# Two linear-attention and gated-MLP layer pairs on one core: block sums asked for later, fold copies moved from VectorE to ScalarE

## The chip, the cores and the metric

The kernel runs on one core of one Trainium2 chip. The metric is the device time of one launch in microseconds, as the median of several launches. All five engines of the core take part: TensorE (PE, with its weight loads listed as PEld), VectorE (DVE), ScalarE (ACT), GpSimd (POOL) and the SyncE queue (SP), which issues most DMAs.

## The reference

The input `x` is 2048 tokens of 1024 features. Four residual layers follow one another, A, B, A, B, numbered 0 to 3 in the kernel; both A layers use the same weights, and so do both B layers.

```python
x = A_x
x = x + _A_ref(_layernorm(x), A_wqkv, A_wo)
x = x + _B_ref(_layernorm(x), B_W_gate, B_W_up, B_W_down)
x = x + _A_ref(_layernorm(x), A_wqkv, A_wo)
x = x + _B_ref(_layernorm(x), B_W_gate, B_W_up, B_W_down)
```

`_A_ref` is linear attention with 32 heads of 32: with `phi(t) = where(t > 0, t + 1, exp(t)) + 1e-6` it forms `kv = phi(k)^T v` per head, divides `phi(q) kv` by `phi(q) . sum(phi(k)) + 1e-6`, and multiplies by `wo`. `_B_ref` is `(relu(x Wg) * (x Wu)) Wd` with 3584 hidden features.

## The kernel before, in words

All tokens lie in SBUF as 16 tiles `x0` to `x15` of 128 tokens by 1024 features. A matmul is 128x128 by 128x512, and a unit of eight of them fills one PSUM bank.

**Layer A.** `project` (L436) makes q and k unit by unit. Once `kv` of all heads is known, it is multiplied into the output weights ahead of any query: `fold_wo(n)` (L630 to L651), n = 0 to 3, runs 16 small matmuls into four PSUM banks (`kv0`, `kv1` and two of the pool `ps3`) and then copies the four banks, i = 0 to 3, into the bf16 tiles `T`. The next call uses the same four banks, so its matmuls wait for these copies. Between two calls one or two `project` units of q run. `phi` (L370) turns a q unit into phi(q): three ACT instructions (L377 to L379) and one of DVE (L385), or one of ACT (L375) and two of DVE (L383, L385). At last `out_unit(sc, j, n2)` (L653) multiplies phi(q), transposed as `pqT`, with `T`: eight matmuls (L657) into a bank of the pool `ps`, which has four, and one DVE addition (L664) onto half of a token tile `x`. An out unit can start when the addition of the fourth unit before it has freed its bank. There are four quarters `sc` of eight out units.

**Between A and B.** While the out units of quarters 1 to 3 run, the first eight token tiles are normed for layer B: statistics (DVE, L154 and L159), 1/sigma (ACT, L161 and L162), a shift (DVE, L186), scaling to f16 (ACT, L188), and a DMA transpose issued by SP (`ln_turn`, L352) into `xnT`, two tiles of four token tiles each. The DMA transposes of `pqT` (L628) stand in the same SP queue, and each waits for GpSimd's scaling (L623).

**Layer B.** The gate and up products are computed with seven block products in place of eight. Four of the seven use sums and differences of blocks of the normed tokens. `sums_x(l, c, j)` (L815 to L827) makes them for one column block: for j = 0 to 3 it takes token tile j from the first `xnT` and token tile 4 + j from the second, and runs four DVE instructions (s1 to s4) into two tiles `s`. The first such product of layer B, `vg` (`mm(w, 5, ...)`, L866), reads the s1 part of all four j. The sums of the weights are read back from DRAM in layer 3, and made by DVE in layer 1 (`make_gu`, L784 to L792), which starts at the end of layer 0.

**What sets the order.** `later` is a list of tasks with due times, counted in ticks; `run` calls `tick` once behind each out unit. DVE and GpSimd have a hand-written order in this part (`manual_schedule`, L714): their instructions stand in the queue as the program text and the due tasks emit them. The order on PE, ACT and SP comes from a scheduler. In quarter `sc == 2` the sums of j = 0 to 3 are due 6, 9, 12 and 15 ticks ahead (L744 to L746). Ticks 1 to 8 follow the out units of quarter 2, ticks 9 to 16 those of quarter 3.

Of the kernel before, what the change touches and what calls it, by code (L numbers as in the profile page):

```python
# [89 lines left out]
class _Net:  # L90
# [318 lines left out]
    def layer_A(self, l, last_ln):  # L409
        nc, G, KT, D = self.nc, self.G, self.KT, self.D  # L410
        ring, later = self.ring, self.later
# [56 lines left out]
        def m_units(d):  # L468
            mt = self.temp([P, D], BF16, name=f"mt{l}_{d}")
            for h in range(H):  # L470
                ps = self.ps3.tile([P, NW], F32, tag="b")
                for t in range(self.ST):
                    nc.tensor.matmul(ps, lhsT=self.xn[l, t][:, d * P:(d + 1) * P],  # L473
                                     rhs=self.pk[l, t][:, h * NW:(h + 1) * NW],
                                     start=(t == 0), stop=(t == self.ST - 1))
                    if t == self.ST // 2 - 1:
                        later.tick()
                nc.scalar.activation(out=mt[:, h * NW:(h + 1) * NW], in_=ps, func=ACT.Copy)
                if h == H - 1:
                    later.at(2, lambda: kv_step(d, mt))  # L480
                later.tick()
# [122 lines left out]
        def z_chain(i):  # L604
            z_mult(*divmod(i, QT))
            if i < 10:
                later.at(2, lambda: z_chain(i + 1))

        def z_mult(sc, j):
            prod = ksum  # L610
            nc.gpsimd.tensor_tensor(out=prod, in0=pq_of[sc, j], in1=zrow, op=ALU.mult)  # L611
            later.at(2, lambda: z_sum(prod, sc, j))
# [17 lines left out]
        def fold_wo(n):  # L630

            n2, a = divmod(n, H)
            if n2 == 0:
                T.append(self.slot(f"T{l}_{a}", [P, 4, D]))
            ps = [pool.tile([P, NW], F32, tag=tag, name=f"fold{l}_{n}_{i}") for i, (pool, tag) in
                  enumerate(((self.kvp, "kv0"), (self.kvp, "kv1"), (self.ps3, "b"), (self.ps3, "b")))]
            wo = ring.get((l, f"o{n2}"))
            for b in range(R):
                g = a * R + b
                for i in range(R):  # L640
                    e = slice(i * HD, (i + 1) * HD)
                    nc.tensor.matmul(ps[i][b * HD:(b + 1) * HD, :], lhsT=kvT[e, g, e],
                                     rhs=wo[e, g, :], start=True, stop=True,
                                     tile_position=(i * HD, b * HD))
            for i in range(R):
                g = a * R + i
                dst = T[g // 4][:, g % 4, n2 * NW:(n2 + 1) * NW]
                if g % 2 or (l and g % 4):
                    nc.scalar.activation(out=dst, in_=ps[i], func=ACT.Copy)
                else:  # L650
                    nc.vector.tensor_copy(out=dst, in_=ps[i])  # L651
# [16 lines left out]
        def column_major(f, q):  # L668
            return [lambda j=j, c=c: f(q, j, c) for c in range(H) for j in range(QT)]

        def row_major(f, q):
            return [lambda j=j, c=c: f(q, j, c) for j in range(QT) for c in range(H)]

        def run(*lists):

            n = max(len(u) for u in lists)
            for i in range(n):
                for u in lists:
                    if i < len(u):
                        u[i]()  # L680
                        later.tick()
# [32 lines left out]
        with self.tc.manual_schedule(engines={mybir.EngineType.DVE, mybir.EngineType.Pool}):  # L714
            q3 = row_major(q_unit, self.NQ - 1)
            out0 = column_major(out_unit, 0)
            if l == 0:
                ring.free_before((l, "v0"))
                later.at(5, z_row)
                later.at(7, lambda: z_chain(0))  # L720
                for d in range(KT):
                    m_units(d)
            else:
                ring.load_to(ring.index((l, "v1")) + 1)
                m_products(q3.pop(0))
                q3.insert(0, lambda: None)
                later.at(1, lambda: self.behind(ring.last, self.bring_back, range(self.NS)))
                for t in range(self.NS, self.ST, 2):
                    later.at(10 + t, lambda t=t: self.behind(self.last_turn, self.bring_back, (t, t + 1)))

            def with_fold(u, i):
                return lambda: (u(), fold_wo(i // 2) if i % 2 == 0 else None)

            run(q3[:2])
            run([with_fold(u, i) for i, u in enumerate(q3[2:] + out0[:1])])
            run(out0[1:3])
            ring.free_slowly((l, "o0"), later, 2)
            for i in range(11, self.ST):
                later.at(1 + 3 * (i - 11), lambda i=i: z_mult(*divmod(i, QT)))
            run(out0[3:])  # L740
            for sc in range(1, self.NQ):
                if sc < 3:
                    self.ln_later(last_ln, sc - 1, 0, 3, 2)
                if sc == 2:  # L744
                    for j in range(QT):
                        later.at(3 * j + 6, lambda j=j: self.sums_x(last_ln, 0, j))  # L746
                if sc == 3 and l == 0:
                    for w in "gu":
                        later.at(8, lambda w=w: self.make_gu(ring.get((last_ln, 0, w, 0)), w, 0))
                run(row_major(out_unit, sc))  # L750
# [313 lines left out]
```

## Time and profile before

| what | before |
|---|---|
| time, median of 3 | 1482.26 us (1481.64 to 1482.26) |
| span of the profiled execution | 1482.7 us |
| PE busy | 1471.9 us, 99% |
| DVE busy | 868.5 us, 59% |
| ACT busy | 517.5 us, 35% |
| POOL busy | 283.8 us, 19% |
| mean granted TensorE clock | 0.999 |
| fold copies, ACT (L649) | 20, median 596 ns |
| fold copies, DVE (L651) | 12, median 681 ns |
| additions of out units, DVE (L664) | 64, median 680 ns |
| block sums, DVE (L824 to L827) | 16 each, about 420 ns each |

The folds of layer 0 end near 175 us and its out units near 237 us of the span. Those of layer 2 run from 900 to 914 us, and its out units from 911.5 to 971.5 us. In a list of instructions in order of time, a row gives the start, the duration, engine, line and operation, output and inputs and a count; the bracket behind it is the time that the engine stood idle before it and what it then waited for.

### The profile page before, as it was taken

Reading aid. Unit: us, or ns where it says so; the run is one execution under the profiler, and the core shown is the slowest. Engines: PE = TensorE matmul, PEld = TensorE weight load, DVE = VectorE, ACT = ScalarE, POOL = GpSimd, SP = SyncE. Lnnn points to the kernel's source line nnn. Section 1 sums busy time; section 2 is a strip of 40 time slices with the busy share of each in tenths; the row PEclk is TensorE's granted clock in tenths of the full one; section 3 lists DMA queues with packets and bytes.
Section 4 is the critical chain, followed back from the end, with each engine's and each line's share of the span. In section 5 each row is a group of like instructions: output and inputs, shape, how many; then the busy total and the mean of one; then the engine's idle time right before and its main releaser. Section 6 shows DMA issues by size and latency. Waiting matters only on the chain.

```text
span 1482.7 us, 18649 instructions
## 1 busy us (share of the span) xinstructions
PE 1471.9 (99%) x7007; PEld 668.5 (45%) x7007; DVE 868.5 (59%) x1491; ACT 517.5 (35%) x927; POOL 283.8 (19%) x190
## 2 busy tenths in 40 slices
PE   9999999999999999999999999999999999999999
PEld 4444444444444444444444444444444444444444
DVE  8995787666594433356379867874445433434632
ACT  5752323333330333340067524343333203333300
POOL 1356540111100011110023475401111000111000
PEclk9999999999999999999999999999999999999999
DMA  9855538444458954445833019984444688444461
GB/s 281 215 169 178 118 58 248 156 143 156 160 182 245 339 180 131 148 131 192 265 100 71 1 36 266 255 266 142 139 145 134 186 245 267 142 142 146 150 208 43
DMA packets 316060, 251.33 MB, mean 170 GB/s; under 512 B 105536, under 2 KB 291136, under 8 KB 315072
## 3 DMA queue, kind: packets, MB, share of 16 engines
q1 hardware_dynamic: 306000, 229.80, 53.2%
q10 hardware_dynamic: 9968, 20.32, 3.6%
q8 instruction: 55, 0.90, 0.3%
q14 instruction: 37, 0.30, 0.1%
HBM read 190.84 MB, written 34.60 MB: 152 GB/s over the span
## 4 chain that ended last, share of the span: by engine, by line
PE 86%; DVE 6%; issue 1%; DMA 0%; ACT 0%; DVEq 0%; ACTq 0%
PE yg L851 10%; PE dy L935 10%; PE yu L851 10%; PE ps L436 7%; PE dv L935 7%; PE dx L935 7%; PE xu L851 6%; PE xg L851 6%; PE ps L473 4%; PE vg L851 3%; PE vu L851 3%; PE zu L851 3%; PE zg L851 3%; PE ps L657 3%; PE my L534 1%; DVE x L664 1%
## 5 line engine op out<-in xcount | busy, mean ns | idle before, releaser
L851 PEld LDWEIGHTS <-w 128*128 128x128 f16 (+1 forms) x3136 | 306.7, 98 | 370.7 <-DVE w L789 1.1
L889 POOL TENSOR_TENSOR h<-m5u,m5g 128x512 f16<-128x512 f32 x56 | 71.2, 1271 | 814.5 <-DVE m5u L885 803.6
L436 PE MATMUL ps<-w,xnT 128*128 128x512 bf16 x1024 | 223.9, 379 | 0.5 <-DVE pq L385 0.3
L935 PEld LDWEIGHTS <-h 128*128 128x128 f16 x1120 | 109.6, 98 | 132.1
L882 DVE TENSOR_TENSOR zg<-yg,m5g 128x512 f32<-128x512 f32 x56 | 39.2, 699 | 204.2 <-PE yg L851 204.2
L436 PEld LDWEIGHTS <-xnT 128*128 128x128 bf16 x1024 | 99.4, 98 | 120.8 <-issue 2.6
L657 PE MATMUL ps<-T,pqT 128*128 128x512 bf16 x512 | 113.2, 383 | 3.1 <-DVE x L664 3.1
L851 PE MATMUL yg<-s,w 128*128 128x512 f16 x448 | 115.1, 379 | 0.0
L851 PE MATMUL xg<-xnT,w 128*128 128x512 f16 x448 | 115.0, 379 | 0.0
L851 PE MATMUL xu<-xnT,w 128*128 128x512 f16 x448 | 115.0, 379 | 0.0
L851 PE MATMUL yu<-s,w 128*128 128x512 f16 x448 | 115.0, 379 | 0.0
L859 ACT ACTIVATE m5g<-m5g 128x512 f32<-128x512 f32 x56 | 35.2, 629 | 200.2 <-DVE m5g L885 200.2
L935 PE MATMUL dy<-w,h 128*128 128x512 f16 x448 | 98.0, 379 | 0.0
L935 PE MATMUL dx<-w,h 128*128 128x512 bf16 x448 | 97.3, 379 | 0.0
L611 POOL TENSOR_TENSOR kvc<-pq,kvc 128x1024 f32<-128x1024 bf16 x32 | 70.4, 2199 | 71.0 <-DVE den L616 56.8
L657 PEld LDWEIGHTS <-pqT 128*128 128x128 bf16 x512 | 50.3, 99 | 65.1 <-issue 6.3
L154 DVE BATCH_NORM_STATS2 stats<-x 128x6 f32<-128x512 f32 (+1 forms) x120 | 76.6, 672 | 1.9 <-DMA x<-in_A_x_dram 1.6
L161 ACT ACTIVATE rstd<-mv,eps 128x1 f32<-128x1 f32 x64 | 18.2, 290 | 164.8 <-DVE mv L159 164.8
L455 POOL TENSOR_TENSOR kvc<-kvc,slab 128x512 f32<-128x512 f32 x46 | 58.3, 1274 | 75.1 <-DVE slab L385 57.3
L862 DVE TENSOR_TENSOR h<-yu,r 128x512 f16<-128x512 f32 x56 | 38.7, 692 | 56.3 <-PE yu L851 56.3
L885 DVE TENSOR_TENSOR m5u<-yu,m5u 128x512 f32<-128x512 f32 x56 | 38.7, 692 | 54.0 <-PE yu L851 52.9
L868 ACT ACTIVATE m5g<-vg 128x512 f32<-128x512 f32 x56 | 33.4, 597 | 98.5 <-PE vg L851 71.0
(127 smaller groups left out, 1982.7 us busy)
## 6 DMA issues: line engine op xcount, KB each, us to landing
w<-in_B_W_gate_dram SPq DMA_DIRECT2D x56, 512.0 KB, 5.9
w<-in_B_W_up_dram SPq DMA_DIRECT2D x56, 512.0 KB, 4.8
w<-td SPq DMA_DIRECT2D x32, 896.0 KB, 4.7
w<-in_B_W_down_dram SPq DMA_DIRECT2D x24, 896.0 KB, 5.0
w<-tg SPq DMA_DIRECT2D x42, 512.0 KB, 6.9
w<-tu SPq DMA_DIRECT2D x42, 512.0 KB, 5.7
w<-in_A_wqkv_dram SPq DMA_DIRECT2D x10, 1024.0 KB, 8.1
away<-x SPq DMA_DIRECT2D x16, 512.0 KB, 4.0
```

The costliest lines, as they stand in the source:

```text
L154: self.nc.vector.bn_stats(out=stats[:, c, :], in_=src[:, c * fmax:(c + 1) * fmax])
L436: nc.tensor.matmul(by_row(ps), lhsT=self.xnT[l, l_q][:, kt, j * P:(j + 1) * P], rhs=w[:, kt, :].rearrange("p (b i d) -> p i b d", i=R, d=H ...
L455: nc.gpsimd.tensor_tensor(out=ksum[:, cols], in0=ksum[:, cols], in1=pk, op=ALU.add)
L473: nc.tensor.matmul(ps, lhsT=self.xn[l, t][:, d * P:(d + 1) * P], rhs=self.pk[l, t][:, h * NW:(h + 1) * NW], start=(t == 0), stop=(t == sel ...
L611: nc.gpsimd.tensor_tensor(out=prod, in0=pq_of[sc, j], in1=zrow, op=ALU.mult)
L657: nc.tensor.matmul(ps, lhsT=pqT[sc][:, g, j * P:(j + 1) * P], rhs=T[g // 4][:, g % 4, n2 * NW:(n2 + 1) * NW], start=(g == 0), stop=(g == G ...
L851: nc.tensor.matmul(ps, lhsT=W[w][m][:, k, :], rhs=A[m][:, k, :], start=start and k == 0, stop=k == 3, skip_group_check=True)
L862: self.last_put = nc.vector.tensor_tensor(out=h[:, b, :], in0=ps, in1=R.pop(b), op=ALU.mult)
L882: nc.vector.tensor_tensor(out=Z[w], in0=Y[w], in1=V[w], op=ALU.add)
L885: nc.vector.tensor_tensor(out=V[w], in0=Y[w], in1=V[w], op=ALU.add)
L889: nc.gpsimd.tensor_tensor(out=h[:, 3, :], in0=V["u"], in1=V["g"], op=ALU.mult)
L935: nc.tensor.matmul(banks[j], lhsT=A(k)[:, j * P:(j + 1) * P], rhs=w[:, i, :], start=start and k == 0, stop=k == self.U - 1, skip_group_che ...
```

## The change

Two edits. The first concerns where the copies of the folded blocks run. In layer 0 nothing changes: odd g on ScalarE, even g on VectorE. In layer 2 (`l` is 2) VectorE had g = 0 and g = 4, which is one of the four copies of each call of `fold_wo`; now all sixteen are on ScalarE. It is meant to take the copies out of VectorE's queue.

The second asks for the sums of blocks later, in both A layers: at ticks 8, 11, 13 and 16 in place of 6, 9, 12 and 15. It is meant to give the DMA transposes more time to land before VectorE reaches the instructions that read them.

```diff
@@ fold_wo
-                if g % 2 or (l and g % 4):
+                if l or g % 2:
                     nc.scalar.activation(out=dst, in_=ps[i], func=ACT.Copy)
                 else:
                     nc.vector.tensor_copy(out=dst, in_=ps[i])
@@ layer_A
                 if sc == 2:
                     for j in range(QT):
-                        later.at(3 * j + 6, lambda j=j: self.sums_x(last_ln, 0, j))
+                        later.at((8, 11, 13, 16)[j], lambda j=j: self.sums_x(last_ln, 0, j))
```

In VectorE's queue the sums of j = 0 and j = 1 move behind two more additions (L664) and a shift (L186), those of j = 2 and j = 3 behind one more addition. The sums of j = 3 now stand behind the last addition of all. In layer 0 one instruction of `make_gu` for the second pair of weight tiles (L789 on `w10`) now stands between s1 and s2 of j = 3, and those of the first pair (`w8`) behind s4. On PE the scheduler's order at the head of layer B changes: in layer 3 it was `vg` first, and is now four matmuls of `xg`, two of `xu`, then `vg`; in layer 1 it was `xg`, `xu`, `vg`, and is now `xg`, `xu`, the second four of `xg`, three of the second four of `xu`, then `vg`. On ACT the last third of a phi (L379) now stands behind an exponential (L375) ahead of the second call's copies, and in SP's queue the transpose of token tile 6 moves ahead of weight loads.

## The prediction

> **What bounds the kernel now.** I first read the page's busy shares: PE is busy 99% of the span, so a change can win only where PE stands still or runs at a reduced clock. So the next view is PE's waits, summed over the whole span (columns: total us, times, longest).
>
> ```profile
> PE ps L657 <- DVE x L664: 3.1, 2, 2.4
> PE fold L642 <- DVE T L651: 1.5, 1, 1.5
> PE vg L851 <- DVE w L789: 0.2, 1, 0.2
> ```
>
> Besides waits at the start and two of 0.3 and 0.5 us, that is all: three places, and both edits aim at them. The timeline of PE shows where each lies.
>
> ```profile
> 226.82 10.52 PE L657 MATMUL ps<-T,pqT 128*128 128x512 bf16 x48 [0.70 <-DVE x L664]
> 239.30 1.04 PE L851 MATMUL vg<-s,w 128*128 128x512 f16 x4 [0.24 <-DVE w L789]
> ...
> 904.33 3.63 PE L436 MATMUL ps<-w,xnT 128*128 128x512 bf16 x16
> 909.42 0.44 PE L642 MATMUL fold<-w,kvc 32*32 32x512 bf16 x16 [1.46 <-DVE T L651]
> ...
> 913.71 43.34 PE L657 MATMUL ps<-T,pqT 128*128 128x512 bf16 x200
> 959.44 12.19 PE L657 MATMUL ps<-T,pqT 128*128 128x512 bf16 x48 [2.39 <-DVE x L664]
> 971.47 1.03 PE L851 MATMUL vg<-s,w 128*128 128x512 f16 x4
> ```
>
> Two things are to be seen: the brackets sum to 0.70 + 0.24 + 1.46 + 2.39 = 4.79 us, and the 48 matmuls behind the longest wait are slow. Before it 200 take 43.34 us, 0.2167 each; the 48 take 971.47 - 959.44 = 12.03 us, where 48 x 0.2167 = 10.40. That is 1.63 us more. The table of windows shows why; its columns are window, length, PE busy and count, granted clock, DMA share, GB/s.
>
> ```profile
> 955.00:957.00 2.00, 2.00 (x10) 1.00 1.00 191
> 957.00:960.00 3.00, 0.61 (x3) 0.91 0.92 176
> 960.00:962.00 2.00, 2.00 (x7) 0.50 1.03 290
> 962.00:964.00 2.00, 2.00 (x9) 0.79 1.27 256
> 964.00:966.00 2.00, 2.00 (x11) 1.00 1.11 271
> ```
>
> The clock was halved for some 3 us after the stop. Why DVE was late shows in its timeline.
>
> ```profile
> 224.61 0.42 DVE L824 TENSOR_TENSOR s<-xnT 128x512 f16<-128x512 f16 x1 [1.61 <-DMA xnT<-xnb]
> ...
> 953.35 0.21 DVE L159 BATCH_NORM_AGGREGATE mv<-stats 128x2 f32<-128x12 f32 x1
> 957.23 0.43 DVE L824 TENSOR_TENSOR s<-xnT 128x512 f16<-128x512 f16 x1 [3.67 <-DMA xnT<-xnb]
> ...
> 958.71 0.68 DVE L664 TENSOR_TENSOR x<-x,ps 128x512 f32<-128x512 f32 x1
> ```
>
> The sums of j = 0 stand at the head of DVE's queue, waiting for a transpose, and the addition that would free a bank stands behind them. The DMA is not what bounds the out units: it is what DVE waited for at the wrong place.
>
> **What the Trainium skill says.** "TensorE: Matmul & The Clock Gate", section "Architectural detail", of the Trainium skill says that DVE and ACT queues are strict first in, first out. The trace agrees: at 957.05 PE had four finished units, DVE idled 3.67 us, and none was added. The same page, section "What's actually happening", says that PE drops to half clock after about 3.4 us of idling, in free-running windows, and needs about as long to come back. Here 2.39 us were enough for 0.50, so the phase of the window matters. The skill's "SBUF — State Buffer", section "Who interferes with whom", says that DVE's two-port forms and GpSimd lock each other out of a shared port pair. I use this only to understand why an L383 at 906.10 lasted 1.87 us where others last 0.42 (GpSimd was busy from 905.77 to 909.95); it held up the copy that the fold waited for.
>
> **The fold copies (layer 2).** Removed from DVE: 4 x 0.68 us; added to ACT: 4 x 0.52 us (three in a row took 1.56 at 905.85). Off DVE nothing is gained directly, since DVE isn't the bound there; what counts is the last copy before each next call. Before, PE was ready for the third call at 907.96 and DVE's copy ended at 909.36. After, the second call's four copies follow each other on ACT. Before, ACT's L377 stood at 903.44, then L378, L379, L375, and three copies from 905.85 to 907.41. The extra copy of the first call moves this by 0.52, and the extra one of the second adds 0.52, so the last ends at about 908.5. The third call then starts when its first bank is free, at about 908.1, and ends at about 908.8 where it ended at 909.79: a gain of 0.9 us. Bounds: 1.46 if ACT keeps up, 0.4 if the reordered L375 waits for its unit and pushes the copies. The second call may wait 0.1 us for the first's fourth copy, which is within that. Behind ACT's copies stand the exponentials of the next q units; DVE's phi then comes about 1 us later at L385 of 905.55, but the banks it frees are needed by PE no sooner than 908.8. The fourth call had 3.5 us of PE work between: hidden.
>
> **The sums in layer 2.** At 953.56 DVE now takes two additions whose units PE had ended at 951.85 and 953.58 (counting back 1.733 us a unit from 957.05), and a shift. It reaches the sums at about 955.0, still waits for the landing at 957.2, and is through at 958.7. By then PE has two freed banks to fill, until 957.05 + 2 x 1.73 = 960.5, and the next addition ends at 959.3. So the 2.39 us go, and with them the stop that cost 1.63 of clock. Further down I ran DVE's new order by the durations of the old rows (0.60 per addition with overlap, 1.45 per four sums, 1.4 per statistics): each addition ends 0.9 to 1.8 us before PE wants its bank. The shift of token tile 6 comes at 954.2 where it was at 959.30, so its transpose can be issued at 958, not 960.81; that of tile 7 at about 962.8, not 965.59.
> The new wait is at the end. PE ends its units at 957.05 + 10.40 = 967.45; the last addition ends at 968.1, s1 of j = 3 at 968.55. PE first has `xg` x4 and `xu` x2, 6 x 0.216 = 1.3 us, and wants `vg` at 968.75: just met. The landing of tile 7, 3.2 to 6.6 us after issue with a median of 4.3 in this stretch, falls at 966 to 969.4, most likely 967.1, ahead of the 968.1 at which DVE asks. If the fold's 0.9 us come off PE but not off the DMA-paced transposes, `vg` waits up to 0.5. I take off 0.3 us. Net: 2.39 + 1.63 - 0.3 = 3.7 us.
>
> **The sums in layer 0.** The same turn removes 0.70: DVE runs two additions from 223.0 in its 1.6 us of idling. PE reaches layer B at 236.5 in place of 237.18. There DVE is the bound for a moment, and one L789 (0.60) for the second weight pair now stands ahead of the first pair's: last addition to 237.1, s1 237.5, L789 on `w10` 238.1, s2 to s4 239.2, L789 on `w8` at 239.8. PE has 15 matmuls of raw products until 239.7, then waits 0.1 for `vg`, 0.2 for the two L789 and L791 of the up weights, and 0.2 for the zg addition. So of 0.70 + 0.24, 0.5 come back: net 0.4, between 0 and 0.9.
>
> **Moved at no cost.** The other sums and shifts in both layers have the same count and durations; they are hidden behind PE's units. Weight loads of layer 3 come up to 1.2 us later in SP's queue, but `w103` was issued at 958.09 and isn't used until some 12 us into layer B. Behind this, layer B has no PE wait on weights or DMA, so the gain stays to the end.
>
> Sum: 0.9 + 3.7 + 0.4 = 5.0 us, so 1482.26 - 5.0 = 1477.2 us.
>
> **Rivals.** (1) Everything is as above, but the launches that are timed didn't have the clock drop: the profiled one has it, and the windows run freely. Then the 1.63 isn't there to win: 1477.2 + 1.6 = 1478.8. For it: 2.39 us is short of the 3.4 that the skill gives. Against it: the three times lie within 0.6 us, so no launch differs from another by 1.6. (2) The waits move: tile 7 lands at the late end, 969.4, `vg` idles about 1.1 us, the fold wins only 0.4, layer 0 nothing: 0.4 + 4.0 - 1.1 - 0.8 more in banks = 2.5, so 1479.8. For it: the DMA share is over 1.0 in the whole stretch. (3) It becomes slower: the sums of j = 3, now behind the last addition, hold up the start of both layers B by some 3 us each, each followed by a halved clock (1.6), while the removed waits give back only 4.8 and 1.6: 2 x 4.6 - 6.4 = +2.8, so about 1485.3. For it: the first product needs all four j. Against it: the scheduler put raw products ahead of `vg`, and landing had over 1 us to spare before.
>
> **How the numbers follow.** The forecast has 0.58, rival 1 0.20, rival 2 0.15, rival 3 0.07. The bound of 0.2% is 3.0 us, at 1479.3 and 1485.2. Faster: all of the forecast, nearly all of rival 1 and little of rival 2, 0.77. Within: most of rival 2 and a part of rival 3, 0.17. Slower: 0.06. The range goes from 1475.6 (all waits gone: 4.79 + 1.63 = 6.4, and some noise) to 1480.4 (beyond rival 2).
>
> **What would show it.** In PE's waits, L657 on L664 should be gone, L642 on T down to about 0.5 us or less and now on ACT. The 48 matmuls ahead of layer 3 should take 10.4 us with the clock at 1.00. DVE should still wait about 2 us for `xnT` in layer 2, to nobody's harm. `vg` of layer 3 should wait less than 0.5 us. I am wrong if PE waits for `vg` by more than a microsecond, or if the clock still drops.

## The result, and the profile after

The changed kernel takes 1478.26 us (median of 6 launches, 1477.22 to 1479.06) against 1482.30 us before (6 launches, 1481.64 to 1483.07). The ratio is 0.9971, with a 95% interval of 0.9958 to 0.9984: 4.0 us less, 0.29%. A second set of five launches (e4) gave 0.9968 (0.9955 to 0.9980), 1477.27 us. The forecast was 1477.2 us.

The spans of the two traces differ by more than the times do, 1482.7 - 1476.4 = 6.3 us. That difference is the main thing to be explained. The answers of the trace come first.

PE's waits of the changed kernel (total us, times, longest): the three rows shown of before are gone. Of what is left, these are the longest; they lie at the start of the kernel and, for L473, at 109 us in layer 0.

```profile
PE idle L246 <- DVE e L243: 1.3, 1, 1.3
PE ps L473 <- DVE slab L385: 0.5, 1, 0.5
PE tp L286 <- DVE x L168: 0.3, 1, 0.3
```

PE's timeline of the changed kernel, folds and out units of layer 2:

```profile
902.99 0.58 PE L642 MATMUL fold<-w,kvc 32*32 32x512 bf16 x16
903.50 3.63 PE L436 MATMUL ps<-w,xnT 128*128 128x512 bf16 x16
907.06 0.70 PE L642 MATMUL fold<-w,kvc 32*32 32x512 bf16 x16
...
911.62 53.70 PE L657 MATMUL ps<-T,pqT 128*128 128x512 bf16 x243
965.16 1.03 PE L851 MATMUL xg<-xnT,w 128*128 128x512 f16 x4
966.02 0.59 PE L851 MATMUL xu<-xnT,w 128*128 128x512 f16 x2
966.45 1.03 PE L851 MATMUL vg<-s,w 128*128 128x512 f16 x4
```

The third call comes right behind its q units, at 907.06. It takes 0.70 us where a call that waits for nothing takes 0.44: with the last of the four copies ending at 907.29 it starts on banks that are free and waits inside for the last, as forecast. The out units run through in one piece, and `vg` follows the raw products without a gap. The windows (window, length, PE busy and count, granted clock, DMA share, GB/s) show the clock at 1.00 where it had been 0.50:

```profile
957.00:960.00 3.00, 3.00 (x16) 1.00 0.89 199
960.00:962.00 2.00, 1.95 (x10) 1.00 1.05 384
```

DVE's timeline of the changed kernel has the wait for the transpose still in it, to nobody's harm, and what I had not valued enough, the shift of token tile 7 (L186 at 958.72) AHEAD of the sums of j = 1:

```profile
954.53 0.43 DVE L824 TENSOR_TENSOR s<-xnT 128x512 f16<-128x512 f16 x1 [1.65 <-DMA xnT<-xnb]
...
958.72 0.21 DVE L186 TENSOR_SCALAR shift<-mv,rstd 128x1 f32<-128x1 f32 x1
...
959.44 0.42 DVE L824 TENSOR_TENSOR s<-xnT 128x512 f16<-128x512 f16 x1
...
965.96 0.42 DVE L824 TENSOR_TENSOR s<-xnT 128x512 f16<-128x512 f16 x1
```

ACT's timeline of the changed kernel: the four copies of the second call end at 907.29. L375 didn't wait for its unit.

```profile
904.15 0.58 ACT L375 ACTIVATE e<-ps 128x512 f32<-128x512 f32 x1
...
905.24 2.05 ACT L649 ACTIVATE T<-fold 128x512 bf16<-128x512 f32 x4
```

### The profile page after: what moved, and what is told of

Read it like the earlier page. It is cut to its first block, busy times and chain, and to the rows that moved or that the text cites. A ratio compares the mean times of both kernels' runs of the same rounds, so it can differ in the third digit from the quotient of the medians.

```text
span 1476.4 us, 18611 instructions
## 1 busy us (share of the span) xinstructions
PE 1468.0 (99%) x6965; PEld 667.7 (45%) x7007; DVE 864.9 (59%) x1487; ACT 518.9 (35%) x931; POOL 283.8 (19%) x190
## 4 chain that ended last, share of the span: by engine, by line
PE 91%; DVE 2%; issue 1%; ACT 0%; DVEq 0%
PE yg L851 10%; PE yu L851 10%; PE dy L935 10%; PE ps L436 8%; PE ps L657 7%; PE dv L935 7%; PE dx L935 7%; PE xu L851 6%; PE xg L851 6%; PE ps L473 4%; PE vg L851 3%; PE zu L851 3%; PE zg L851 3%; PE vu L851 3%; PE my L534 1%; PE mv L534 1%
## 5 line engine op out<-in xcount | busy, mean ns | idle before, releaser
L935 PEld LDWEIGHTS <-e 128*128 128x128 f16 x448 | 43.8, 98 | 52.9
```

The costliest lines, as they stand in the source:

```text
L935: nc.tensor.matmul(banks[j], lhsT=A(k)[:, j * P:(j + 1) * P], rhs=w[:, i, :], start=start and k == 0, stop=k == self.U - 1, skip_group_che ...
```

## The experiments

To compare traces I cut PE's time at four marks: the first fold call of layer 0, the first and the fourth fold call of layer 2, and the `vg` of layer 3's second weight pair. "Head" is what lies between the first two (it contains the sums of layer 0), "folds" the next stretch, "tail" the last (it contains the sums of layer 2). All in us. Spans are not compared as a whole, because launches differ by up to 3.3 us before the first mark (it lies at 169.2 to 172.5 us in the traces, whatever the edit). The clock column counts launches whose mean granted clock over the whole span was 0.999 or less, so that a half-rate stretch is somewhere in them; it does not say where.

| kernel | head | folds | tail | time ratio to before (95%) | launches with a clock drop anywhere |
|---|---|---|---|---|---|
| before, as traced ahead of the prediction | 729.31 | 13.40 | 70.21 | | |
| e1 before again | 729.54 | 13.40 | 68.24 | 0.9999 (0.9991 to 1.0007) | 1 of 13 |
| e2 fold copies only | 729.52 | 12.25 | 68.53 | 0.9987 (0.9981 to 0.9994) | 1 of 21 |
| e3 sums only | 728.21 | 13.40 | 65.99 | 0.9978 (0.9969 to 0.9986) | 0 of 12 |
| changed kernel | 728.54 | 12.19 | 66.00 | 0.9971 (0.9958 to 0.9984) | 0 of 6 |
| e4 changed again | 728.49 | 12.26 | 65.99 | 0.9968 (0.9955 to 0.9980) | 0 of 5 |
| e5 j = 0 at tick 5, layer 2 | 729.28 | 13.39 | 71.19 | 1.0022 (1.0014 to 1.0030) | 12 of 14 |
| e6 j = 0 at tick 7, layer 2 | 729.38 | 13.40 | 68.49 | 0.9999 (0.9991 to 1.0007) | 2 of 13 |
| e7 j = 0 at tick 8, layer 2 | 729.35 | 13.40 | 67.83 | 1.0001 (0.9991 to 1.0011) | 4 of 14 |
| e8 changed, one copy, j = 3 at 15 | 728.20 | 12.87 | 66.36 | 0.9981 (0.9973 to 0.9989) | 4 of 13 |
| e9 j = 0 and 1 later, layer 2 | 729.33 | 13.40 | 66.23 | 0.9986 (0.9979 to 0.9992) | 1 of 21 |
| e10 j = 1 later, layer 2 | 729.58 | 13.39 | 67.90 | 1.0002 (0.9994 to 1.0010) | 2 of 13 |
| e11 j = 0 and 3 later, layer 2 | 729.51 | 13.40 | 66.82 | 0.9989 (0.9982 to 0.9996) | 0 of 21 |
| e12 changed, j = 3 at 15 in layer 0 | 728.20 | 12.25 | 65.99 | 0.9966 (0.9954 to 0.9979) | 0 of 5 |

### Was the traced launch of before like the timed ones? (e1)

> The kernel before, unchanged, launched often, to see span and clock of each launch. Theory A (the halved clock after the 2.39 us stop comes only in some launches): most launches have a span near 1480.4 us (1482.3 less the 1.85 us by which time exceeds span elsewhere) at clock 1.000, a few have 1482 to 1483 us at 0.999. Theory B (the clock drops in every launch): all launches have spans near 1482.5 us at 0.999, and the 2.3 us between the traced span difference (6.3) and the timed one (4.0) has another cause.

Theory A holds. Of the 146 launches of the kernel before in these comparisons, on three chips, 19 had the clock drop (1 of 13 and 3 of 40, 6 of 44, 9 of 49); the median spans of the comparison launches were 1480.5, 1480.9 and 1480.6 us. There had been a sign of it: the launch that was profiled ahead of the prediction took 1484.57 us, 2.3 us above the median of the three timed ones, and its span (1482.7) alone exceeds that median, while in every launch of these comparisons the time is 1.7 to 1.9 us longer than the span. PE's timeline of e1 has the stop, but shorter, and another wait at the head of layer 3 that the first trace did not have:

```profile
957.43 10.52 PE L657 MATMUL ps<-T,pqT 128*128 128x512 bf16 x47 [1.42 <-DVE x L664]
968.45 1.04 PE L851 MATMUL vg<-s,w 128*128 128x512 f16 x4 [0.50 <-DVE s L824]
```

So the tail costs 68.24 us in this launch and 70.21 in the one that the prediction was made from. The difference, 1.97 us, is 0.97 of a longer stop and 1.63 of half clock, less the 0.50 at `vg`; 0.1 is left over. It is most of the 2.3 us by which the traced difference exceeds the timed one; the rest (0.3 us) is within the spread of the launches.

The 19 launches need not have lost their clock in layer 2. In the traced launch of e6, which is one of those with the drop, the half rate lies at 8.6 to 12.0 us of the span, behind a stop of 1.97 us at the start of the kernel, and the clock stayed at 1.00 in layer 2. So at most 19 of 146 had it behind the stop in layer 2; the launch lists alone can't say how many.

The traces do show which stop is followed by half clock. In all 14 the granted clock changes only on a grid of 3.413 us. In the trace of before it changes at 7.12 us (to full), 959.44 (to half), 962.86 (to full) and, after the last matmul, at 1481.68 (to half): 279, 1 and 152 steps apart. Below are windows cut on that grid around the longest stop, first of before, then of e10 (a later experiment with a stop of 1.72 us):

```profile
956.03:959.44 3.41, 1.02 (x5) 1.00 0.99 182
959.44:962.85 3.41, 3.41 (x9) 0.50 0.95 293
```

```profile
954.39:957.80 3.41, 1.70 (x8) 1.00 0.93 174
957.80:961.21 3.41, 3.41 (x17) 1.00 1.04 299
```

In before the whole stop of 2.39 us falls into one window, and the next runs at half clock. In e10 PE idles 1.71 us of its window, and the next runs at full clock. Over all windows of the 14 traces, from the first change of the clock to the last, each in which PE idled 2.03 us or more is followed by half clock (17 of them, 14 behind the last matmuls of the kernel), and none in which it idled 1.72 us or less. By these figures a stop of 1.42 us as in e1 could not halve the clock wherever it fell.

### Each part alone (e2, e3, e4)

```diff
# e2: fold copies only
-                if g % 2 or (l and g % 4):
+                if l or g % 2:
# e3: sums only
-                        later.at(3 * j + 6, lambda j=j: ...)
+                        later.at((8, 11, 13, 16)[j], lambda j=j: ...)
# e4: both
```

> Only the copies of the second layer's folds move to ScalarE; sums are due as before. The theory of two separate edits: PE's wait of L642 on L651 goes, about 1.2 us less than before (1481.1), and the waits for the transposes stay at 0.7 and about 2.4 us, since the chain that issues the transposes moves along with PE. Rival (the transposes are paced by DMA traffic that does not move): PE comes to the sums 1.2 us earlier and waits 1.2 us longer, 3.6 us in layer 2, and the time is that of before.

> Only the due times of the sums change; VectorE keeps its fold copies. Theory: PE's waits of L657 on L664 go in both layers, L642 on L651 stays at 1.46 us, the clock stays at 1.00; from the traces 2.39 + 0.2 + 0.8 = 3.4 us, and 1.6 us more in those launches of before that had the halved clock: timed 1478.9 by theory A (drop in few launches), 1477.3 by theory B (in all).

> Both edits, the changed kernel unchanged, to be compared on the same chip. If the two edits add up: gain of the fold alone plus gain of the sums alone, about 4.2 us by theory A, 1478.1.

The parts add up. The folds alone shorten their stretch by 13.40 - 12.25 = 1.15 us and leave the tail at 68.5, 0.3 us longer than in e1; the rival, in which PE only meets the transposes sooner, would have put 1.15 onto the tail. The transposes moved with PE: the sums of j = 0 started 1.2 us earlier than in e1 (954.03 for 955.23), PE's longest wait on L664 was 1.58 for 1.42. The sums alone take 1.3 us off the head and 2.25 off the tail against e1. Times: -1.9, -3.3 and -4.7 us of 1482.3, with intervals of about 0.9 us or more to either side. From the traces, against e1, the changed kernel is about 1.0 (head) + 1.14 to 1.21 (folds) + 2.25 (tail) = 4.4 to 4.5 us shorter.

### How far ahead the sums of j = 0 may stand (e5, e6, e7)

Layer 2 alone, all other due times as before:

```diff
-                        later.at(3 * j + 6, lambda j=j: ...)
+                        later.at((5 if l and j == 0 else 3 * j + 6), lambda j=j: ...)   # e5; 7 in e6, 8 in e7
```

> The kernel before, but the sums of j = 0 in layer 2 are due one out unit EARLIER (tick 5, not 6); all else as before. Theory (the additions behind the waiting sums set PE's stop; one out unit of 1.73 us for each tick): the stop of L657 on L664 grows from 1.4 to 2.4 us to about 3.2 to 4.1 us, the clock falls to half behind it in most launches (0.999 in the launch list), and the time is 1.7 to 3.4 us above before: 1484.0 to 1485.7. Rival (the length of the stop is set by the landing alone, or the clock drop is chance): time within 0.5 us of before, clock 1.000 in nine of ten launches as before.

> The kernel before, but the sums of j = 0 in layer 2 are due one out unit later (tick 7); all else as before. Theory: one addition more ahead of the sums frees one bank, worth 1.73 us, so the stop of 1.4 to 2.4 us shrinks to 0 to 0.7, the clock stays at 1.00, and time is 1.4 to 2 us below before: 1480.5. A second step (tick 8) then has little left to win. Rival (both out units are needed): the stop stays above 1 us.

> The kernel before, but the sums of j = 0 in layer 2 are due two out units later (tick 8), as in the changed kernel; j = 1 to 3, layer 0 and the folds as before. Theory (only the wait at j = 0 costs time): the whole gain of the sums in layer 2, about 2.2 us, so 1480.1; the shift of token tile 6 comes earlier too, and with it the late landing of tile 7, so layer 3's first vg doesn't wait. Rival (the later j count too): less than half of it, with PE waiting for the sums of j = 1 to 3.

One tick earlier behaved as the theory said: a stop of 3.42 us, half clock behind it, 12 of 14 launches with a drop where before had 6 of 44 on the same chip, and 3.3 us more time. PE's timeline of e5, and its windows:

```profile
959.46 13.86 PE L657 MATMUL ps<-T,pqT 128*128 128x512 bf16 x56 [3.42 <-DVE x L664]
```

```profile
958.00:960.00 2.00, 0.54 (x2) 0.84 0.90 169
960.00:962.00 2.00, 2.00 (x7) 0.50 0.94 286
```

Later did not. With j = 0 alone at tick 8, just as in the changed kernel, the stop is gone and yet no time is gained (ratio 1.0001; the tail of the trace is 0.4 us shorter than in e1). The wait has moved to the head of layer 3, as the rival had it. PE's timeline of e7, then DVE's:

```profile
912.45 53.70 PE L657 MATMUL ps<-T,pqT 128*128 128x512 bf16 x248
967.82 1.04 PE L851 MATMUL vg<-s,w 128*128 128x512 f16 x4 [1.67 <-DVE s L824]
```

```profile
954.87 0.43 DVE L824 TENSOR_TENSOR s<-xnT 128x512 f16<-128x512 f16 x1 [1.17 <-DMA xnT<-xnb]
...
958.38 0.37 DVE L824 TENSOR_TENSOR s<-xnT 128x512 f16<-128x512 f16 x1
...
960.40 0.21 DVE L186 TENSOR_SCALAR shift<-mv,rstd 128x1 f32<-128x1 f32 x1
...
967.34 0.42 DVE L824 TENSOR_TENSOR s<-xnT 128x512 f16<-128x512 f16 x1 [2.19 <-DMA xnT<-xnb]
```

Between the landing of token tile 4 (954.87) and the shift of token tile 7 (960.40) stand two sets of sums. From that shift it takes 6.9 us of scaling and transpose until the sums of j = 3 can start. At tick 7 (e6) the same waiting is spread out: 0.43 and 0.45 us among the out units and 1.14 at `vg`, 2.02 in all where e1 had 1.42 + 0.50 = 1.92.

The theory that the prediction shares with e6 and e7 falls here. One tick earlier the missing bank does lengthen the loss (e5). From tick 6 on, the additions behind the sums of j = 0 set where PE waits, but no longer how much it waits in all. A chain through DVE is then proposed as what sets that; the next three runs test it: landing of tile 4, sums of j = 0, addition, statistics of tile 7, sums of j = 1, addition, shift of tile 7, scaling, transpose, sums of j = 3, `vg`.

### What shortens the chain (e9, e10, e11)

```diff
-                        later.at(3 * j + 6, lambda j=j: ...)
+                        later.at((8, 11, 12, 15)[j] if l else 3 * j + 6, lambda j=j: ...)   # e9
+                        later.at((6, 11, 12, 15)[j] if l else 3 * j + 6, lambda j=j: ...)   # e10
+                        later.at((8, 9, 12, 16)[j] if l else 3 * j + 6, lambda j=j: ...)    # e11
```

> The kernel before, with j = 0 at tick 8 and j = 1 at tick 11 in layer 2 only (j = 2 and 3 at 12 and 15 as before). Revised theory: what bounds this stretch is a chain on VectorE from the landing of token tile 4 over the sums of j = 0, the statistics and the shift of token tile 7, its scaling, its transpose and the sums of j = 3 to vg; the sums of j = 1 (1.45 us) stand inside it before the shift. So vg's wait of 1.67 us (j = 0 alone) falls to about 0.2, no stop among the out units, clock 1.00 in nearly all launches: time 1.6 us below before. Rival (j = 1 is of no account, vg waits for the DMA): vg still waits over 1 us and the time is that of before.

> The kernel before, with only j = 1 at tick 11 in layer 2 (j = 0 at 6, j = 2 and 3 at 12 and 15). Revised theory: the stop of 1.4 us among the out units stays, since the sums of j = 0 stay ahead of the additions, and vg's wait (0.5) goes: 0.5 us or less below before. Rival (the chain is all that counts): the full 1.5 us are gained with j = 1 alone.

> The kernel before, with j = 0 at tick 8 and j = 3 at tick 16 in layer 2 (j = 1 and 2 at 9 and 12 as before). Revised theory: PE has six raw products (1.3 us) ahead of vg, as in the changed kernel, so of the 1.67 us that vg waits with j = 0 alone about 0.4 to 0.6 are left, and the time is about 1.2 us below before. Rival (the landing moves later with the sums): vg waits 1 us or more.

All three came out as the chain says. With j = 0 and j = 1 later, `vg` follows the out units at once, the tail is 66.23 us, 2.0 less than in e1, and the time 2.1 us less. PE's and DVE's timelines of e9:

```profile
912.33 53.70 PE L657 MATMUL ps<-T,pqT 128*128 128x512 bf16 x248
966.09 1.04 PE L851 MATMUL vg<-s,w 128*128 128x512 f16 x4
```

```profile
959.07 0.21 DVE L186 TENSOR_SCALAR shift<-mv,rstd 128x1 f32<-128x1 f32 x1
959.80 0.42 DVE L824 TENSOR_TENSOR s<-xnT 128x512 f16<-128x512 f16 x1
```

With the landing of tile 4 at the same place (954.88 for 954.87), the shift comes at 959.07 in place of 960.40: 1.33 us, about one set of sums. The transpose of tile 7 is issued 1.32 us sooner (960.59 for 961.91) and lands 1.74 us sooner (the sums of j = 3 start at 965.60 for 967.34); so 0.4 us of it is a shorter transpose, not the chain. With j = 1 later alone (e10) `vg` doesn't wait, but the stop among the out units is there, 1.72 us, and the tail is only 0.34 us shorter. Only both together pay. In e11 the chain is about as long as in e7 (`vg` starts 56.0 us behind the fourth fold call, for 55.7), but PE does six raw products first:

```profile
966.16 1.03 PE L851 MATMUL xg<-xnT,w 128*128 128x512 f16 x4
968.28 1.04 PE L851 MATMUL vg<-s,w 128*128 128x512 f16 x4 [0.66 <-DVE s L824]
```

0.66 us are left of 1.67, and the tail is 1.0 us shorter than in e7. So two places of the chain are shown by experiment: the sums of j = 1 inside it, and what PE has to do at its end. The other links are read from the traces and were not moved one by one.

### Retouches (e8, e12)

```diff
# e8, on the changed kernel
-                if l or g % 2:
+                if g % 2 or (l and (g % 4 or n == 1)):
# e8 (15 in both layers); e12 (16 if l else 15, folds as changed)
-                        later.at((8, 11, 13, 16)[j], ...)
+                        later.at((8, 11, 13, 15)[j], ...)
```

> The changed kernel with two retouches: only the second call's copy of i = 0 goes to ScalarE (g % 2 or g % 4 or n == 1 in layer 2; VectorE keeps one copy of calls 1, 3 and 4), and the sums of j = 3 are due at tick 15. Theory: only that one copy held up PE, and without an extra copy of the first call ScalarE is 0.52 us sooner, so from the first to the fourth call of layer 2's folds 11.9 to 12.4 us pass (13.40 before, 12.19 to 12.26 with all four moved); at the head of layer 1 the L789 of the second weight pair no longer stands between the sums, 0 to 0.4 us less. Together 0 to 0.6 us below the changed kernel, 1477.0 to 1478. Rival (each copy on VectorE delays something): the fold stretch goes back towards 13.4.

> The changed kernel with j = 3 at tick 15 in layer 0 and 16 in layer 2. Layer 2 as in the changed kernel: no PE wait, 66.0 us from the fourth fold call to vg of the second pair. Head of layer 1: the sums no longer surround a weight instruction, 0 to 0.3 us less. Time 1477.3 to 1478.3 on a chip where before has 1482.3, not distinguishable from the changed kernel; a retouch worth more would show a shorter stretch from the first fold of layer 0 to that of layer 2 (728.5 us).

My theory of a single copy falls. In e8 the third call is at once ready, but the fourth waits for the copy that DVE kept; PE's timeline:

```profile
907.40 0.48 PE L642 MATMUL fold<-w,kvc 32*32 32x512 bf16 x16
...
912.33 0.44 PE L642 MATMUL fold<-w,kvc 32*32 32x512 bf16 x16 [0.89 <-DVE T L651]
```

The fold stretch is 12.87 us, worse than the 12.25 with all copies on ACT. `vg` waits 0.19 us with j = 3 at 15, and 4 of 13 launches had a clock drop. The traced launch isn't one of them and has no stop in layer 2 that is long enough, so where PE stopped in those four stays open; e6 shows that it can be the start of the kernel. e12 keeps tick 16 in layer 2 and takes 15 in layer 0. The head is 728.20 in e8 and in e12, which both have tick 15 in layer 0, and 0.3 us longer in the two traces of the changed kernel; but e3, with tick 16 in both layers, has 728.21 too. By time it can't be told from the changed kernel.

## Why the prediction was right, point by point

- **What bounds the kernel.** Right: PE's few waits were all that there was to win, and with both edits they are gone.
- **The fold copies.** Right in mechanism, a quarter too small: 0.9 us forecast, 1.15 to 1.21 measured. The copies on ACT ended at 907.29, which is about 0.3 us sooner than my 908.5 once the 0.9 us are taken off by which this trace is ahead. The fourth call is hidden, as I had said, but only because its copies moved too: with the third call's copy left on DVE it waits 0.89 us (e8), which I had not seen.
- **The sums in layer 2.** The net of 3.7 us was the term that failed. It took 2.39 us of stop and 1.63 of half clock for what every launch loses. In e1 the stop is 1.42, with 0.50 at `vg`, and the clock drops in at most 19 of 146 launches. The argument that I set against rival 1, that the three times lie within 0.6 us, said nothing of the launch that was profiled: it is a fourth one, of 1484.57 us. The tail won 2.25 us against e1, and 4.2 only against the launch that I had. Rival 1, to which I gave 0.20, had this right for the clock, and its 1478.8 is 0.5 us from the first set of launches (1478.26); but my 1477.2 is 0.1 us from the second (1477.27), so it is the clock of the launches that decides, not the times. That the phase of the window matters, as I had inferred, is what the grid of the clock changes shows. That the stop itself was longer than usual in the traced launch, neither case had.
- **Why the stop goes.** Incomplete. I credited the two additions ahead of the sums of j = 0. e7 has just these, and gains no time. What pays is that with j = 1 later the shift of tile 7 comes a set of sums sooner (e9), and that raw products stand ahead of `vg` (e11). Both were in the changed order that I followed by hand (transpose of tile 7 at about 962.8 for 965.59, raw products 1.3 us), so the number for `vg` was right, below 0.5 us, but the credit went to the wrong part of the edit.
- **The sums in layer 0.** Mechanism right, size off: 0.4 us forecast, about 1.0 measured (head 729.5 to 728.5). The stop there is 0.91 to 1.01 us in five of the traces with the early sums and 0.68 to 0.79 in three more, where mine had 0.70: it too varies from launch to launch, and against e1 (0.95) next to nothing of the 0.5 that I took off for the inserted L789 is seen.
- **Rivals 2 and 3.** No wait at `vg`; neither came true. (Rival 3's own sum, +2.8, gives 1485.1 and not 1485.3; nothing hangs on it.) But e7 shows that rival 2's mechanism is real: with j = 1 left where it was, 1.67 us are lost at `vg`.
- **The sum.** 5.0 us forecast; 4.0 and 4.7 us measured in two sets of launches. The layer 2 term was 1.4 us too large, folds and layer 0 were 0.9 us too small. That the total came this close is luck: errors of opposite sign cancelled.

## What to carry to other kernels

A wait that ends first on an in-order engine shows where the time is lost, not what the loss is tied to: before moving the waiting instruction, follow the chain from the landing through that engine to the next thing that PE needs, and see what of it the move takes out. Small stops of a busy PE vary from launch to launch; before a traced stop and a clock drop behind it are entered at full size, look at more than one launch, or at least compare the profiled launch's own time with the median, and give the difference its own line. A total that adds up is no proof of its terms. Move all copies that stand between dependent calls, or the wait turns up one call later.

## What the runs showed of the hardware

- The clock falls by windows, not by the length of a stop alone. Clock changes lie on a grid of 3.413 us within each of the 14 traces; windows with 2.03 us or more of PE idling are followed by half clock, those with 1.72 us or less are not, and none lies between. Stops of 2.39 us (before), 3.42 us (e5) and 1.97 us (e6, with 0.13 more in the same window) were followed by it, stops of 1.42 to 1.72 us (e1, e2, e10) not. The Trainium skill ("TensorE: Matmul & The Clock Gate", section "What's actually happening") speaks of a free-running window of 3413 ns, which agrees with this grid, and of half clock after at least one idle window of about 3.4 us; here 2.03 us of a window were enough, and the measurement decides.
- One window at half clock cost 1.63 us in before (48 matmuls in 12.03 us for 10.40) and 1.56 us in e5 (56 matmuls in 13.69 us for 12.13).
- Two launches of the same program differed by 1 us in the stop on a DMA transpose (2.39 and 1.42 us), and one of them had a wait of 0.50 us at `vg` that the other didn't have.
